# The last 64 rows of w_down as 128 half rows, in a one-token decoder block

## The chip, the core and the metric

The kernel runs on one core of a Trainium2 chip. A core has five instruction streams: TensorE (PE in the profile, with PEld for its weight loads), VectorE (DVE), ScalarE (ACT), GpSimd (POOL) and SyncE (SP), which here issues nearly all transfers. Sixteen DMA engines move the data between HBM and SBUF. The metric is the device time of one execution in microseconds, as the median of several runs. The kernel before took 206.41 us (three runs, 206.30 to 206.46).

## What is computed

One token (x, 640 values) goes through attention over a cache of 4096 positions in 32 heads, and then through a gated MLP with 1728 hidden columns:

```
h  = x + softmax(q k^T / sqrt(128)) v @ wo          q = layernorm(x) @ wq
g  = layernorm(h) @ w_gate                          w_gate, w_up: 640 x 1728
u  = layernorm(h) @ w_up
h2 = h + (gelu(g) * u) @ w_down                     w_down: 1728 x 640
```

All inputs are bfloat16. The caches are 64 of the 84 MB that are read; w_gate, w_up and w_down are 2.2 MB each.

## The kernel before

The kernel is written out by hand for the five engines. A small helper (class Sched) collects each engine's instructions in the order in which the code names them, with the semaphore waits of each; nothing is reordered after that. All large transfers stand in one queue, SP's, and are worked off in its order.

The first 170 us stream the caches. For eight groups of four heads, VectorE multiplies keys by the query (L296), TensorE folds the products (L305), VectorE reduces them (L312), ScalarE exponentiates (L344), and TensorE sums the values (L351). K and V have two buffers each; SP waits for a buffer to come free before it issues the next load (L222, L231).

The weights of the second half stand behind the caches in the same queue, into buffers that are free by then: wo in four pieces, w_gate and w_up in two each (L384), then w_down. 1728 hidden columns are 13 full slices of 128 and a remainder of 64 (FREM). L395 loads the remainder, 64 rows of w_down, on partitions 0 to 63 of slice 13 of wd_sb. L400 then loads the 13 full slices in four parts of 6, 4, 2 and 1 slices (WD_PARTS), each on 128 partitions; within a part of n slices, a partition holds n rows that follow each other in memory.

The MLP uses the hidden columns in the same layout. Function up (L444 to L457) multiplies five chunks of the 640 inputs by the 14 slices, 70 matmuls into one column of a PSUM tile for each slice, once for w_gate (pg) and once for w_up (pu). The remainder's matmuls have 64 columns of weights and fill rows 0 to 63 alone; the other rows of pg and pu are set to zero at the start (L192, L193). VectorE and ScalarE then form gelu(g) * u in hm, one column for each slice (L461 to L470).

The down projection (L472 to L480) takes 4 matmuls for each slice, one for each quarter of the 640 outputs, into four rows of pd (a PSUM tile that the profile calls pf). The remainder comes first, with 64 rows, then the 13 slices as their parts land. VectorE copies the result (L481), and SP stores it (L482).

TensorE runs its instructions in order, so a matmul that waits for a part of w_down holds up all behind it.

Of the kernel before, what the change touches and what calls it, by code (L numbers as in the profile page):

```python
# [5 lines left out]
FP32 = mybir.dt.float32  # L6
BF16 = mybir.dt.bfloat16
ALU = mybir.AluOpType
ACTF = mybir.ActivationFunctionType
AX = mybir.AxisListType  # L10

D = 640
# [3 lines left out]
DF = 1728  # L16
# [7 lines left out]
NG = H // HG  # L24
# [4 lines left out]
NFT = 13  # L29
NF = NFT + 1  # L30
WD_PARTS = (6, 4, 2, 1)
# [5 lines left out]
FREM = DF - NFT * 128  # L37
# [67 lines left out]
def bass_sequential_preLN__gqa_block_cached__glu_gated_geglu__decode_kernel(  # L105
# [12 lines left out]
    S = Sched(nc)  # L118

    def sb(name, shape, dt):  # L120
        return nc.alloc_sbuf_tensor(name, shape, dt)
# [7 lines left out]
    def over(name, base, shape):  # L129
        return nc.alloc_sbuf_tensor_at(name, shape, BF16, offset=nc.lookup_mloc(base).addr)  # L130
# [3 lines left out]
    wg_sb = over("wg_sb", kbuf[NG % 2], [128, NC_D, DF])  # L134
    wu_sb = over("wu_sb", kbuf[(NG + 1) % 2], [128, NC_D, DF])
    wd_sb = over("wd_sb", vbuf[NG % 2], [128, NF, D])
# [21 lines left out]
    hln = sb("hln", [128, NC_D], BF16)  # L158
# [6 lines left out]
    r_t = sb("r_t", [128, NF], FP32)  # L165
    gu = sb("gu", [128, NF], FP32)
    hm = sb("hm", [128, NF], BF16)
    o_sb = sb("o_sb", [128, D // 4], BF16)
    hx = sb("hx", [128, 32, NC_D], FP32)
    m32 = sb("m32", [128, 32], FP32)  # L170
# [3 lines left out]
    I32 = sb("I32", [128, 128], FP32)  # L174
# [8 lines left out]
    pz = nc.alloc_psum_tensor("pz", [128, 512], FP32)  # L183
    pg = nc.alloc_psum_tensor("pg", [128, 512], FP32)
    pu = nc.alloc_psum_tensor("pu", [128, 512], FP32)
# [3 lines left out]
    t_onebf = S.op("vector", lambda v: v.memset(ones_bf[:, :], 1.0))  # L189
    t_p4 = [S.op("vector", lambda v, i=i: v.memset(P4[i][:, :, :], 0.0)) for i in range(2)]  # L190
    t_rs = S.op("vector", lambda v: v.memset(RS[:, :], 0.0))
    t_pg = S.op("vector", lambda v: v.memset(pg[:, 0:NF], 0.0))  # L192
    t_pu = S.op("vector", lambda v: v.memset(pu[:, 0:NF], 0.0))  # L193
    t_i32 = S.op("gpsimd", lambda g: g.affine_select(
        I32[:, :], ones[:, :], pattern=[[1, 128]], compare_op=ALU.is_equal,
        fill=0.0, base=0, channel_multiplier=-1), [t_one])
# [3 lines left out]

    t_e4 = S.op("vector", lambda v: v.reduce_sum(
        e4[:, :], I32[:, :].rearrange("p (j i) -> p j i", j=4), axis=AX.X), [t_i32])
    t_m32 = S.op("vector", lambda v: v.reduce_sum(
        m32[:, :], I32[:, :].rearrange("p (j i) -> p i j", j=4), axis=AX.X))
    t_sel = None
# [13 lines left out]
    kfree, vfree = [None] * NG, [None] * NG  # L219
# [27 lines left out]
    def layernorm(src, t_src, o, dst, ps, beside=None):  # L247
        a = S.op("vector", lambda v: v.tensor_mul(sq[:, :], src[:, :], src[:, :]), [t_src])
        S.op("vector", lambda v: v.reduce_sum(st[:, o:o + 1], src[:, :], axis=AX.X))
        b = S.op("vector", lambda v: v.reduce_sum(st[:, o + 1:o + 2], sq[:, :], axis=AX.X), [a])  # L250
        c = S.op("tensor", lambda t: t.matmul(ps[:, 0:2], ones[:, :], st[:, o:o + 2],  # L251
                                              start=True, stop=True), [b, t_one])
        if beside is not None:
            beside()
        q = 6 * (o // 2)
        d = S.op("vector", lambda v: v.tensor_scalar(
            ln[:, q:q + 1], ps[:, 0:1], inv_d, 0.0, ALU.mult, ALU.add), [c])
        e = S.op("vector", lambda v: v.tensor_scalar(
            ln[:, q + 1:q + 2], ln[:, q:q + 1], ln[:, q:q + 1], -EPS, ALU.mult, ALU.add), [d])
        f = S.op("vector", lambda v: v.tensor_scalar(  # L260
            ln[:, q + 2:q + 3], ps[:, 1:2], inv_d, ln[:, q + 1:q + 2], ALU.mult, ALU.subtract), [e])
        k = S.op("scalar", lambda a: a.activation(ln[:, q + 3:q + 4], ln[:, q + 2:q + 3], ACTF.Ln), [f])  # L262
        m = S.op("scalar", lambda a: a.activation(
            ln[:, q + 4:q + 5], ln[:, q + 3:q + 4], ACTF.Exp, scale=-0.5), [k])
        return S.op("vector", lambda v: v.tensor_scalar(  # L265
            dst[0], dst[1], ln[:, q:q + 1], ln[:, q + 4:q + 5], ALU.subtract, ALU.mult), [m])
# [113 lines left out]
    def pieces(slot, dst, src, cuts, waits):  # L380
        toks = []
        for i in range(len(cuts) - 1):
            lo, hi = cuts[i], cuts[i + 1]
            tok = S.dma("sync", "%s%d" % (slot, i), lambda s, lo=lo, hi=hi: s.dma_start(  # L384
                dst[:, lo:hi, :], src[:, lo:hi, :]), waits)
            toks += [tok] * (hi - lo)
        return toks
# [3 lines left out]
    d_wg = pieces("wg", wg_sb, B_w_gate[:, :].rearrange("(p c) n -> p c n", c=NC_D),  # L391
                  [0, 3, 5], [kfree[NG - 2]])
    d_wu = pieces("wu", wu_sb, B_w_up[:, :].rearrange("(p c) n -> p c n", c=NC_D),
                  [0, 3, 5], [kfree[NG - 1]])
    d_wdr = S.dma("sync", "wdr", lambda s: s.dma_start(  # L395
        wd_sb[0:FREM, NFT, :], B_w_down[NFT * 128:DF, :]), [vfree[NG - 2]])
    d_wd = []
    for i, n in enumerate(WD_PARTS):
        s0 = len(d_wd)
# [10 lines left out]
    b = None  # L410
    for j in range(4):
        b = S.op("tensor", lambda t, j=j: t.matmul(
            pq[:, 0:32], sel[:, j, :], aH[:, 32 * j:32 * j + 32], start=(j == 0), stop=(j == 3)),
            [a, t_sel, t_qb[NG - 1]], token=(j == 3))
# [4 lines left out]
    for c in range(H):  # L419
        for cc in range(NC_D):  # L420
            last = c == H - 1 and cc == NC_D - 1
            b = S.op("tensor", lambda t, c=c, cc=cc, last=last: t.matmul(  # L422
                pp[:, cc:cc + 1], wo_sb[:, c, cc::NC_D], aP[:, c:c + 1],
                start=(c == 0 and cc == 0), stop=last, skip_group_check=True),
                [t_ap, d_wo[c]], token=last)
# [3 lines left out]
    pd = pf[1]  # L429
    NQ = D // 4  # L430
# [10 lines left out]
    t_hln = layernorm(h32, t_h, 2, (hln[:, :], h32[:, :]), pz, residual)  # L441


    def up(ps, w, d_w, t0):  # L444
        b = None
        for c in range(NC_D):
            for s in range(NF):
                first = c == 0 and s == 0
                last = c == NC_D - 1 and s == NF - 1
                rows, cols = FREM, slice(NFT * 128, DF)  # L450
                if s < NFT:
                    b0, n, k = WD_COLS[s]
                    rows, cols = 128, slice(b0 + k, b0 + 128 * n, n)
                b = S.op("tensor", lambda t, s=s, c=c, rows=rows, cols=cols, first=first, last=last: t.matmul(
                    ps[0:rows, s:s + 1], w[:, c, cols], hln[:, c:c + 1],
                    start=first, stop=last, skip_group_check=True), [t_hln, d_w[c], t0], token=last)
        return b  # L457

    t_g = up(pg, wg_sb, d_wg, t_pg)
    t_u = up(pu, wu_sb, d_wu, t_pu)  # L460
    a = S.op("vector", lambda v: v.tensor_copy(g_t[:, :], pg[:, 0:NF]), [t_g])  # L461
    a = S.op("vector", lambda v: v.tensor_mul(t1[:, :], g_t[:, :], g_t[:, :]), [a])
    a = S.op("vector", lambda v: v.tensor_mul(t2[:, :], t1[:, :], g_t[:, :]), [a])
    a = S.op("vector", lambda v: v.scalar_tensor_tensor(
        out=t3[:, :], in0=t2[:, :], scalar=GELU_C1, in1=g_t[:, :], op0=ALU.mult, op1=ALU.add), [a])
# [3 lines left out]
    a = S.op("vector", lambda v: v.tensor_mul(gu[:, :], g_t[:, :], r_t[:, :]), [a])  # L469
    t_hm = S.op("vector", lambda v: v.tensor_mul(hm[:, :], gu[:, :], pu[:, 0:NF]), [a, t_u])  # L470

    order = [NFT] + list(range(NFT))  # L472
    for i, s in enumerate(order):
        kk = FREM if s == NFT else 128
        for j in range(4):
            last = i == NF - 1
            b = S.op("tensor", lambda t, s=s, j=j, kk=kk, last=last: t.matmul(  # L477
                pd[32 * j:32 * j + 1, 0:NQ], hm[0:kk, s:s + 1], wd_sb[0:kk, s, j * NQ:(j + 1) * NQ],
                start=False, stop=last, skip_group_check=True),
                [t_hm, d_wd[s]], token=(last and j == 3))  # L480
    t_o = S.op("vector", lambda v: v.tensor_copy(o_sb[:, :], pd[:, 0:NQ]), [b])  # L481
    d_o = S.dma("sync", "out", lambda s: s.dma_start(  # L482
        out[0, 0, :].rearrange("(j i) -> j i", j=4), o_sb[0:128:32, :]), [t_o])
# [32 lines left out]
```

## Time and profile before

The profiled execution took 206.16 us, 0.25 us less than the median.

| | |
|---|---|
| median of the runs | 206.41 us |
| the profiled execution | 206.16 us |
| its span, first to last instruction | 204.9 us |
| busy: PE, DVE, ACT, POOL | 132.3, 103.4, 24.4, 2.2 us |
| bytes read from HBM | 84.23 MB, 411 GB/s over the span |
| L454 (up), 128 columns: weight load, matmul | 127 ns, 178 ns |
| L454 (up), 64 columns: weight load, matmul | 127 ns, 212 ns |
| L477 (down): weight load, matmul | 79 ns, 338 ns (medians) |
| L395 (remainder): issue, issue to landing | 0.62 us, 25.3 us |

Busy times of TensorE add up pipelined instructions, so its matmuls overlap. A row of a timeline gives the start, the duration, the engine, the line and the operation, and in brackets how long the engine sat idle before it and what ended that. The rows of DMA in slices are the share of time in which the core's 16 DMA engines were busy, and the GB/s that they moved.

### The profile page before, as it was taken

The numbers are of one execution on the slowest core, as the hardware profiler recorded it, in microseconds if no ns is written. First come the engines' busy times: TensorE is split into PE (matmuls) and PEld (weight loads), VectorE is DVE, ScalarE is ACT, GpSimd is POOL, SyncE is SP. The second block draws the span as 40 slices with busy tenths as digits, with TensorE's granted clock in tenths as the row PEclk, the third lists the DMA queues.
The fourth block names the chain that finished last, engine by engine and source line by source line (L and its number), as shares of the span: only waits on it lengthen the run. The fifth ranks groups of instructions, "written<-read, shape, count | busy, mean of one in ns | idle before, by whom it ended". The sixth has DMA issues, their size and how long they took to land.

```text
span 204.9 us, 3982 instructions
## 1 busy us (share of the span) xinstructions
PE 132.3 (65%) x1847; PEld 77.5 (38%) x1847; DVE 103.4 (50%) x118; ACT 24.4 (12%) x86; POOL 2.2 (1%) x11
## 2 busy tenths in 40 slices
PE   0003057656897668785968478858776958676884
PEld 0002012222562363254326223713272228676672
DVE  2003088699579537935772777187627950101120
ACT  2001000040230040022005000500040004000000
POOL 3000000000000000000000000000000000000000
PEclk9999999999979955995799579757975797555555
DMA  7999999999999999999999999999999999999991
GB/s 256 432 432 409 416 486 422 416 416 457 448 413 416 429 453 429 416 419 440 435 435 422 413 441 448 419 419 429 441 448 419 400 413 431 429 402 421 405 358 62
DMA packets 4712, 84.48 MB, mean 412 GB/s; under 512 B 664, under 2 KB 856, under 8 KB 1880
## 3 DMA queue, kind: packets, MB, share of 16 engines
q1 hardware_dynamic: 4552, 84.23, 96.8%
q8 instruction: 14, 0.23, 0.5%
q10 hardware_dynamic: 144, 0.00, 0.0%
q14 instruction: 2, 0.02, 0.0%
HBM read 84.23 MB, written 0.00 MB: 411 GB/s over the span
## 4 chain that ended last, share of the span: by engine, by line
DMA 61%; DVE 20%; PE 13%; SPq 4%; issue 1%
DMA kbuf<-in_A_k_cache_dram 50%; DVE prod L296 16%; DMA wd_sb<-in_B_w_down_dram 10%; PE pf L305 10%; SPq L400 4%; DVE sc L312 4%; PE po L351 2%; PE pm L331 0%; PE pf L477 0%; DVE mx L329 0%; PE pz L370 0%; PE pm L337 0%; SPq L212 0%; DVE mrow L334 0%; DVE o_sb L481 0%
## 5 line engine op out<-in xcount | busy, mean ns | idle before, releaser
L305 PE MATMUL pf<-prod,Ibf 128*128 128x512 bf16 x256 | 73.9, 447 | 36.8 <-DVE prod L296 36.7
L296 DVE TENSOR_TENSOR prod<-kbuf,qb 128x4096 bf16<-128x4096 bf16 x32 | 72.4, 2282 | 27.5 <-DMA kbuf<-in_A_k_cache_dram 26.9
L305 PEld LDWEIGHTS pf<-prod,Ibf 128*128 128x128 bf16 x256 | 26.5, 111 | 81.1 <-DVE prod L296 45.9
L312 DVE TENSOR_REDUCE sc<-pf 128x32 f32<-128x512 f32 x32 | 21.9, 686 | 21.6 <-PE pf L305 21.6
L351 PE MATMUL po<-P,vbuf 128*128 128x4 bf16 x1024 | 27.9, 165 | 1.6 <-issue 1.6
L351 PEld LDWEIGHTS po<-P,vbuf 128*128 128x128 bf16 x1024 | 27.4, 100 | 1.8 <-issue 1.7
L344 ACT ACTIVATE P<-sc,nb 32x128 bf16<-32x128 f32 x32 | 18.6, 580 | 0.9
L285 ACT CAST qb<-pq 128x128 bf16<-128x128 f32 x8 | 2.1, 265 | 103.4 <-PE pq L281 103.4
L251 PE MATMUL pz<-st,ones 128*128 128x2 f32 x4 | 1.2, 364 | 17.5 <-DVE st L250 17.5
L422 PE MATMUL pf<-aP,wo_sb 128*128 128x1 bf16 x160 | 7.0, 179 | 2.3 <-issue 1.8
L344 ACT ACTIVATION_READ_ACCUMULATOR P<-sc,nb 32x1 f32 x32 | 8.1, 253 | 0.0
L422 PEld LDWEIGHTS pf<-aP,wo_sb 128*128 128x128 bf16 x160 | 6.7, 131 | 2.6 <-issue 2.0
L251 PEld LDWEIGHTS pz<-st,ones 128*128 128x128 f32 x4 | 1.0, 313 | 17.6 <-DVE st L250 17.6
L268 DVE CAST x<-x_sb 128x5 f32<-128x5 bf16 x1 | 0.2, 171 | 13.9 <-DMA x_sb<-in_A_x_dram 13.9
L281 PE MATMUL pq<-wq_sb,xb 128*32 128x128 bf16 x160 | 5.7, 232 | 1.7 <-DVE xb L265 1.7
L331 PE MATMUL pm<-I,mx 128*1 128x128 f32 x16 | 3.0, 271 | 4.6 <-DVE mx L329 4.6
L281 PEld LDWEIGHTS pq<-wq_sb,xb 128*32 128x32 bf16 x160 | 4.2, 100 | 4.8 <-issue 3.0
L337 PE MATMUL pm<-mrow,ones 1*128 1x4 f32 x16 | 3.0, 258 | 3.0 <-DVE mrow L334 3.0
L426 DVE TENSOR_TENSOR h<-x,pf 128x5 f32<-128x5 f32 x1 | 0.2, 161 | 9.1 <-PE pf L422 9.1
L262 ACT ACTIVATE ln<-ln 128x1 f32<-128x1 f32 x2 | 0.4, 202 | 35.0 <-DVE ln L260 35.0
L340 ACT ACTIVATE nb<-pm 128x4 f32<-128x4 f32 x8 | 1.4, 173 | 26.5 <-PE pm L337 26.5
L337 PEld LDWEIGHTS pm<-mrow,ones 1*128 1x128 f32 x16 | 2.3, 182 | 5.3 <-DVE mrow L334 5.3
(59 smaller groups left out, 38.2 us busy)
## 6 DMA issues: line engine op xcount, KB each, us to landing
kbuf<-in_A_k_cache_dram SPq DMA_DIRECT2D x8, 4096.0 KB, 27.1
vbuf<-in_A_v_cache_dram SPq DMA_DIRECT2D x7, 4096.0 KB, 29.3
wq_sb<-in_A_wq_dram SPq DMA_DIRECT2D x1, 5120.0 KB, 15.2
wo_sb<-in_A_wo_dram SPq DMA_DIRECT2D x2, 1920.0 KB, 26.6
vbuf<-in_A_v_cache_dram SPq DMA_DIRECT2D x1, 2048.0 KB, 16.0
vbuf<-in_A_v_cache_dram SPq DMA_DIRECT2D x1, 1536.0 KB, 19.3
wg_sb<-in_B_w_gate_dram SPq DMA_DIRECT2D x1, 1296.0 KB, 32.5
wu_sb<-in_B_w_up_dram SPq DMA_DIRECT2D x1, 1296.0 KB, 30.1
```

The costliest lines, as they stand in the source:

```text
L251: c = S.op("tensor", lambda t: t.matmul(ps[:, 0:2], ones[:, :], st[:, o:o + 2], start=True, stop=True), [b, t_one])
L281: tok = S.op("tensor", lambda t, hh=hh, c=c, n0=n0: t.matmul(pq[hh * PPH:(hh + 1) * PPH, 0:DH], xb[:, c, :], wq_sb[:, c, n0:n0 + DH], star ...
L285: t_qb[g] = S.op("scalar", lambda a: a.copy(qb[:, g, :], pq[:, 0:DH]), [tok])
L296: return S.op("vector", lambda v: v.tensor_tensor(out=prod[n % NPR][:, :, :], in0=kbuf[g % 2][:, s * RP:(s + 1) * RP, :], in1=qb[:, g, :]. ...
L305: fold_done[n] = S.op("tensor", lambda t, j=j: t.matmul(pf[n % 2][:, :], Ibf[:, :], prod[n % NPR][:, :, j * W:(j + 1) * W], start=(j == 0) ...
L312: red_done[n] = S.op("vector", lambda v: v.reduce_sum(sc[g % 2][:, s * RP:(s + 1) * RP], pf[n % 2][:, :].rearrange("p (r w) -> p r w", r=R ...
L331: b = S.op("tensor", lambda t: t.matmul(pm[0:1, 0:128], mx[:, g:g + 1], I32[:, :], start=True, stop=True), [a, t_i32, t_exp[g - 1] if g el ...
L337: d = S.op("tensor", lambda t: t.matmul(pm[:, 256:256 + HG], ones[0:1, :], mrow[0:1, g * HG:(g + 1) * HG], start=True, stop=True), [c])
L344: t_exp[g] = S.op("scalar", lambda a, lo=lo, hi=hi, h=h, hh=hh: a.activation(P4[g % 2][lo:hi, :, hh], sc[g % 2][lo:hi, :], ACTF.Exp, bias= ...
L351: t_pv[g] = S.op("tensor", lambda t, r=r: t.matmul(po[:, g * HG:(g + 1) * HG], vbuf[g % 2][:, r, :], P4[g % 2][:, r, :], start=(r == 0), s ...
L400: tok = S.dma("sync", "wd%d" % i, lambda s, s0=s0, n=n: s.dma_start(wd_sb[:, s0:s0 + n, :], B_w_down[128 * s0:128 * (s0 + n), :].rearrange ...
L422: b = S.op("tensor", lambda t, c=c, cc=cc, last=last: t.matmul(pp[:, cc:cc + 1], wo_sb[:, c, cc::NC_D], aP[:, c:c + 1], start=(c == 0 and ...
```

## The change

The remainder of w_down is loaded as 128 half rows of 320 values: row r's first half lies on partition 2r, its second half on partition 2r+1. So that the hidden columns can meet it there, the remainder's slice in up is now 128 columns wide: it takes the last 128 columns of w_gate and w_up, of which the first 64 belong to slices that are there already. All rows of pg and pu are now written, and the memsets at the start go.

Of the last column of hm, rows 64 to 127 hold the remainder's 64 values. A new matmul with a 0/1 matrix (twice) puts each of them on two neighbouring partitions, in a column of pz. A multiply on VectorE with a parity mask (hpar) makes two columns of it, hr: one with zeros on odd partitions, one with zeros on even ones. The first goes with the two quarters of the output that the first half rows hold, the second with the other two. The four matmuls of the remainder now come after the first part's 24, not ahead of them.

```diff
--- before.py
+++ after.py
@@ -165,6 +165,9 @@
     r_t = sb("r_t", [128, NF], FP32)
     gu = sb("gu", [128, NF], FP32)
     hm = sb("hm", [128, NF], BF16)
+    hr = sb("hr", [128, 2], BF16)
+    hpar = sb("hpar", [128, 2], FP32)
+    twice = sb("twice", [128, FREM, 2], BF16)
     o_sb = sb("o_sb", [128, D // 4], BF16)
     hx = sb("hx", [128, 32, NC_D], FP32)
     m32 = sb("m32", [128, 32], FP32)
@@ -189,8 +192,6 @@
     t_onebf = S.op("vector", lambda v: v.memset(ones_bf[:, :], 1.0))
     t_p4 = [S.op("vector", lambda v, i=i: v.memset(P4[i][:, :, :], 0.0)) for i in range(2)]
     t_rs = S.op("vector", lambda v: v.memset(RS[:, :], 0.0))
-    t_pg = S.op("vector", lambda v: v.memset(pg[:, 0:NF], 0.0))
-    t_pu = S.op("vector", lambda v: v.memset(pu[:, 0:NF], 0.0))
     t_i32 = S.op("gpsimd", lambda g: g.affine_select(
         I32[:, :], ones[:, :], pattern=[[1, 128]], compare_op=ALU.is_equal,
         fill=0.0, base=0, channel_multiplier=-1), [t_one])
@@ -200,6 +201,10 @@
 
     t_e4 = S.op("vector", lambda v: v.reduce_sum(
         e4[:, :], I32[:, :].rearrange("p (j i) -> p j i", j=4), axis=AX.X), [t_i32])
+    S.op("vector", lambda v: v.reduce_sum(
+        hpar[:, :], I32[:, :].rearrange("p (r h) -> p h r", h=2), axis=AX.X))
+    t_tw = S.op("vector", lambda v: v.tensor_copy(
+        twice[:, :, :], I32[:, 128 - FREM:128].unsqueeze(2).to_broadcast([128, FREM, 2])))
     t_m32 = S.op("vector", lambda v: v.reduce_sum(
         m32[:, :], I32[:, :].rearrange("p (j i) -> p i j", j=4), axis=AX.X))
     t_sel = None
@@ -393,7 +398,7 @@
     d_wu = pieces("wu", wu_sb, B_w_up[:, :].rearrange("(p c) n -> p c n", c=NC_D),
                   [0, 3, 5], [kfree[NG - 1]])
     d_wdr = S.dma("sync", "wdr", lambda s: s.dma_start(
-        wd_sb[0:FREM, NFT, :], B_w_down[NFT * 128:DF, :]), [vfree[NG - 2]])
+        wd_sb[:, NFT, 0:D // 2], B_w_down[NFT * 128:DF, :].rearrange("r (h n) -> (r h) n", h=2)), [vfree[NG - 2]])
     d_wd = []
     for i, n in enumerate(WD_PARTS):
         s0 = len(d_wd)
@@ -441,23 +446,23 @@
     t_hln = layernorm(h32, t_h, 2, (hln[:, :], h32[:, :]), pz, residual)
 
 
-    def up(ps, w, d_w, t0):
+    def up(ps, w, d_w):
         b = None
         for c in range(NC_D):
             for s in range(NF):
                 first = c == 0 and s == 0
                 last = c == NC_D - 1 and s == NF - 1
-                rows, cols = FREM, slice(NFT * 128, DF)
+                part = w[:, c, DF - 128:DF]
                 if s < NFT:
                     b0, n, k = WD_COLS[s]
-                    rows, cols = 128, slice(b0 + k, b0 + 128 * n, n)
-                b = S.op("tensor", lambda t, s=s, c=c, rows=rows, cols=cols, first=first, last=last: t.matmul(
-                    ps[0:rows, s:s + 1], w[:, c, cols], hln[:, c:c + 1],
-                    start=first, stop=last, skip_group_check=True), [t_hln, d_w[c], t0], token=last)
+                    part = w[:, c, b0 + k:b0 + 128 * n:n]
+                b = S.op("tensor", lambda t, s=s, c=c, part=part, first=first, last=last: t.matmul(
+                    ps[:, s:s + 1], part, hln[:, c:c + 1],
+                    start=first, stop=last, skip_group_check=True), [t_hln, d_w[c]], token=last)
         return b
 
-    t_g = up(pg, wg_sb, d_wg, t_pg)
-    t_u = up(pu, wu_sb, d_wu, t_pu)
+    t_g = up(pg, wg_sb, d_wg)
+    t_u = up(pu, wu_sb, d_wu)
     a = S.op("vector", lambda v: v.tensor_copy(g_t[:, :], pg[:, 0:NF]), [t_g])
     a = S.op("vector", lambda v: v.tensor_mul(t1[:, :], g_t[:, :], g_t[:, :]), [a])
     a = S.op("vector", lambda v: v.tensor_mul(t2[:, :], t1[:, :], g_t[:, :]), [a])
@@ -469,15 +474,24 @@
     a = S.op("vector", lambda v: v.tensor_mul(gu[:, :], g_t[:, :], r_t[:, :]), [a])
     t_hm = S.op("vector", lambda v: v.tensor_mul(hm[:, :], gu[:, :], pu[:, 0:NF]), [a, t_u])
 
-    order = [NFT] + list(range(NFT))
+    b = S.op("tensor", lambda t: t.matmul(
+        pz[:, 32:33], twice[:, :, :], hm[:, NFT:NF], start=True, stop=True), [t_hm, t_tw])
+    t_hr = S.op("vector", lambda v: v.tensor_tensor(
+        out=hr[:, :], in0=hpar[:, :], in1=pz[:, 32:33].to_broadcast([128, 2]), op=ALU.mult), [b])
+
+    def down(s, j):
+        if s == NFT:
+            return hr[:, j // 2:j // 2 + 1], wd_sb[:, NFT, j % 2 * NQ:(j % 2 + 1) * NQ]
+        return hm[:, s:s + 1], wd_sb[:, s, j * NQ:(j + 1) * NQ]
+
+    order = list(range(WD_PARTS[0])) + [NFT] + list(range(WD_PARTS[0], NFT))
     for i, s in enumerate(order):
-        kk = FREM if s == NFT else 128
         for j in range(4):
             last = i == NF - 1
-            b = S.op("tensor", lambda t, s=s, j=j, kk=kk, last=last: t.matmul(
-                pd[32 * j:32 * j + 1, 0:NQ], hm[0:kk, s:s + 1], wd_sb[0:kk, s, j * NQ:(j + 1) * NQ],
+            b = S.op("tensor", lambda t, s=s, j=j, last=last: t.matmul(
+                pd[32 * j:32 * j + 1, 0:NQ], *down(s, j),
                 start=False, stop=last, skip_group_check=True),
-                [t_hm, d_wd[s]], token=(last and j == 3))
+                [t_hr if s == NFT else t_hm, d_wd[s]], token=(last and j == 3))
     t_o = S.op("vector", lambda v: v.tensor_copy(o_sb[:, :], pd[:, 0:NQ]), [b])
     d_o = S.dma("sync", "out", lambda s: s.dma_start(
         out[0, 0, :].rearrange("(j i) -> j i", j=4), o_sb[0:128:32, :]), [t_o])

```

twice and hpar are built from the identity matrix at the start. The order of the transfers in SP's queue, the number of bytes and the other parts of w_down stay as they were.

## The prediction

> **What bounds the kernel now.** I read the page's slices first, then the chain of waits, then the last microseconds as a timeline, and last the DMA rate in stretches.
>
> ```profile
> span 204.9 us, 3982 instructions
> ...
> DMA  7999999999999999999999999999999999999991
> ...
> q1 hardware_dynamic: 4552, 84.23, 96.8%
> q8 instruction: 14, 0.23, 0.5%
> ```
>
> The DMA row is full from the second slice to the next to last: 84 MB go in without a pause, and engines' work counts only where no transfer covers it. The end of the chain of waits says which transfer the end hangs on:
>
> ```profile
> 180.74 21.34 DMA wd_sb<-in_B_w_down_dram
> 202.12 0.73 PE pf L477 x12
> 202.87 0.32 DVE o_sb L481
> ```
>
> The last parts of w_down are on their way for 21 us, then 12 matmuls, a copy and the store end the kernel. The timeline of the tail shows how far each engine is from that path:
>
> ```profile
> 198.80 0.17 DVE L470 TENSOR_TENSOR hm<-gu,pu 128x14 bf16<-128x14 f32 x1 [2.05 <-PE pu L454]
> 199.02 0.09 PEld L477 LDWEIGHTS pf<-wd_sb,hm 64*1 64x1 bf16 x4 [0.42 <-DVE hm L470]
> 199.03 0.30 PE L477 MATMUL pf<-wd_sb,hm 64*1 64x160 bf16 x4 [0.33 <-DVE hm L470]
> 199.78 0.63 PEld L477 LDWEIGHTS pf<-wd_sb,hm 128*1 128x1 bf16 x24 [0.67 <-DMA wd_sb<-in_B_w_down_dram]
> ...
> 201.31 0.36 PEld L477 LDWEIGHTS pf<-wd_sb,hm 128*1 128x1 bf16 x16 [0.90 <-DMA wd_sb<-in_B_w_down_dram]
> ...
> 202.12 0.10 PEld L477 LDWEIGHTS pf<-wd_sb,hm 128*1 128x1 bf16 x8 [0.45 <-DMA wd_sb<-in_B_w_down_dram]
> 202.52 0.09 PEld L477 LDWEIGHTS pf<-wd_sb,hm 128*1 128x1 bf16 x4 [0.30 <-DMA wd_sb<-in_B_w_down_dram]
> ```
>
> Each of the four parts of w_down (6, 4, 2 and 1 slices) lets TensorE wait: 0.67, 0.90, 0.45 and 0.30 us. So the end moves only if the last part lands at another time. When it lands is a matter of the rate, in stretches:
>
> ```profile
> core 0: us, PE busy (x) PEld busy (x) DVE busy (x) ACT busy (x) POOL busy (x), PEclk, DMA share, GB/s
> 185.00:193.50 8.50, 6.05 (x114) 5.18 (x113) 1.40 (x8) 0.41 (x2) 0.47 (x1) 0.50 1.01 418
> 193.50:195.50 2.00, 2.00 (x43) 1.93 (x42) 0.42 (x3) 0.00 (x0) 0.00 (x0) 0.50 1.04 359
> 195.50:196.50 1.00, 1.00 (x21) 0.96 (x19) 0.65 (x4) 0.22 (x1) 0.00 (x0) 0.50 0.96 391
> 196.50:197.50 1.00, 0.99 (x21) 0.89 (x21) 0.22 (x2) 0.00 (x0) 0.00 (x0) 0.50 0.98 330
> ...
> 198.00:198.50 0.50, 0.50 (x14) 0.48 (x14) 0.00 (x0) 0.00 (x0) 0.00 (x0) 0.50 1.09 435
> ```
>
> The DMA engines are busy all through (0.96 to 1.04), but from 193.5 to 195.5 and again from 196.5 to 197.5 they move 359 and 330 GB/s instead of 418. The trace's records of single packets say the same: for 40 us before, a packet takes its size's usual time within 2%, save where an instruction fetch shares its engine; in these two stretches every packet on every engine takes 1.1 to 1.5 times that. Both stretches follow the transfer that the change remakes, the 64 rows of L395: its 64 packets of 1280 B start from 192.9 to 195.0 on eleven engines and from 196.2 to 196.7 on the other five, each time some 0.5 us before the dip. The last part of w_down has packets of 1280 B too, on 128 partitions (198.3 us on): there the rate is 435 and the packets take their usual 55 ns. So size is not the cause; what sets this transfer apart is that it writes 64 partitions.
>
> **The change part by part.**
> *The transfer of the last rows.* Same 80 KB at the same place in the queue, as 128 packets of 640 B over all partitions. What the dips cost now: (418-359)x2 + (418-391)x1 + (418-330)x1 = 233 KB not moved, or 0.56 us at 418 GB/s. From the packet records, the six engines that end last lost 0.48 to 0.58 us of packet time in the dips; I take 0.50, since those set the end. If the dips go, the last landing moves from 202.47 to about 201.97. If the partitions are not their cause, the gain is 0.
> Against it stands the smaller packet. Packets of 320, 1280 and 2560 B take 18, 55 and 102 ns in the records, those of one engine following at 3 ns less; 640 B interpolates to 30. Each engine then spends 8x27 = 216 ns instead of 4x52 = 208: +0.01 us. The bounds are 8x18 = 144 (a 320 B packet's price, -0.06) and 8x52 = 416 (a 1280 B packet's, +0.21). I take +0.02, since both neighbours lie on one line.
>
> [...]
> [...]
>
> *The queue.* On SP nothing is passed or reordered; the one instruction has twice the packets. SP's issues of L400 already stretch to 5.69 us behind a full queue, so the four behind it may be issued later: four more packets per engine are at most half of an eight-packet part, and the parts ahead of it land 2 to 5 us apart, so up to 2.5 us. The last is issued at 182.6 and lands 19.9 us later; this is hidden by the queue's depth, at zero, and would cost only beyond that.
> *The up projections.* Ten of 140 matmuls have 128 columns instead of 64. By form the two weight loads take 127 ns each, the matmuls 178 and 212 (the narrow ones longer): between -10x0.034 and +0.05 us, taken as 0, as TensorE is done at 198.7 and waits for the first part until 199.78. With the gain that part lands near 199.25, and the path below still comes first.
> *The new matmul and multiply.* After hm (198.97) TensorE duplicates the last column into pz: one weight load and matmul, by L454's rows about 0.25 us, where the four narrow matmuls stood (0.30). It ends by 199.3; behind it on PE stand the 24 of the first part, delayed by at most 0.05 us. VectorE's product of two columns from pz costs 0.16 to 0.22 us (L256 and L260, which read pz), so hr is there by 199.6. Nothing else stands behind it on DVE until L481. The four matmuls that need it now come after the 24, which take 0.97 us and end near 200.3: 0.7 us of slack. They then run 0.30 us to 200.6, before the second part's landing at about 200.8. If this cover of 0.2 us were gone, the 16 behind them would start late, with 0.8 us to the third part's landing to make it up.
> *Start.* Two memsets of 0.07 us go; a reduction (0.27 to 0.37, as L201 and L203) and a copy of 128x128 (0.17 to 0.44, as L188 and L265) come. DVE idles 13.91 us until x lands at 16.2: zero.
>
> *Sum.* -0.50 + 0.02 = -0.48 us. The profiled execution took 206.16 (span 204.9, 1.26 around it): 205.68. The median of the three runs is 0.25 higher, so 206.41 - 0.48 = 205.93. The bounds: -0.56 - 0.06 = -0.62 and, with nothing gained and the dear packet, +0.21.
>
> **The rivals.**
> *The dips stay* (the source side or the start of w_down's stream makes them). For it: the engines read the same 5 KB pieces from the same places, and the packets of the first part of w_down start only 0.2 us after those of the rows. Against it: engines stay on that first part from 195.5 to 196.5 at 391, and the next dip awaits the five late engines' packets of the remainder. Time 206.41 + 0.02 = 206.43.
> *They go only in part*, say to the 0.19 us that 80 KB take at 418 GB/s: one such transfer's own time. Time 206.24. Against it: all engines slow, for over 2 us in all.
> *Half rows are dear and the dips stay:* 640 B at the 1280 B price, 206.62.
> *Slower: an instruction fetch on a late engine.* Queue 8's 14 fetches of 16 KB each hold one DMA engine 1.0 to 1.1 us (packet records). The one at 199.06 falls on an engine that would have ended 1.1 us before the last. The change puts two instructions into TensorE's stream just there; if the fetch falls on one of the five last engines instead, the last landing is 1.1 us later: -0.48 + 1.09 = +0.6, 207.0. It decides as soon as the engine that is hit has less than 0.6 us (1.09 - 0.48) of lead. Against it: the stream up to that point has the same instructions, so the same engine should be next.
>
> **How the numbers follow.** A measurement tells 0.2% (0.41 us) from no change. Dips gone: 0.66, own range 205.65 to 206.1, of it 0.50 beyond 0.41 us and 0.16 short of it. In part: 0.11. Stay: 0.14. Dear half rows: 0.04. Fetch: 0.05. Faster is 0.50, same 0.16 + 0.11 + 0.14 + 0.04 = 0.45, slower 0.05. The range runs from 205.65 to 206.5: it takes in the dips that stay (206.43) and leaves out the last two cases and the far tails.
>
> **What would show it.** Right: from 193.5 to 197.5 the rate stays near 418; the last weight load of the down projection starts near 202.0 instead of 202.52, its four waits remain, and the four matmuls of the half rows start without one for DVE. Wrong: 330 to 360 GB/s in the same stretches (partitions aren't the cause); a wait for hr in TensorE's row; or a late landing with an undisturbed rate (a fetch on a late engine). The prediction is most at risk where the gain is real but 0.3 us, just short of what can be told.

## The result

The changed kernel takes 205.77 us (median of nine runs, 205.55 to 206.00), the kernel before 206.28 in runs beside it. The ratio is 0.9974 with a 95% interval of 0.9964 to 0.9984: 0.54 us faster, between 0.33 and 0.74. The forecast was 205.93, 0.48 us faster.

First the DMA rate of the changed kernel, in the stretches in which the kernel before had its two dips. The last column is GB/s.

```profile
core 0: us, PE busy (x) PEld busy (x) DVE busy (x) ACT busy (x) POOL busy (x), PEclk, DMA share, GB/s
185.00:193.50 8.50, 6.08 (x131) 5.29 (x130) 1.40 (x8) 0.41 (x2) 0.47 (x1) 0.50 1.02 422
193.50:195.50 2.00, 1.30 (x35) 1.22 (x34) 1.15 (x7) 0.22 (x1) 0.00 (x0) 0.50 0.99 410
195.50:196.50 1.00, 0.78 (x23) 0.70 (x21) 0.14 (x1) 0.00 (x0) 0.00 (x0) 0.50 1.07 437
196.50:197.50 1.00, 0.84 (x21) 0.85 (x22) 0.00 (x0) 0.00 (x0) 0.00 (x0) 0.50 0.99 412
```

The dips are gone: 410, 437 and 412 GB/s where 359, 391 and 330 stood. Reckoned as in the prediction, (422-410)x2 + (422-437)x1 + (422-412)x1 = 19 KB or 0.05 us are left of the 0.56.

Then the tail of the changed kernel as a timeline:

```profile
197.96 0.17 DVE L475 TENSOR_TENSOR hm<-gu,pu 128x14 bf16<-128x14 f32 x1 [2.33 <-PE pu L459]
198.19 0.10 PEld L477 LDWEIGHTS pz<-hm,twice 128*128 128x128 bf16 x1 [0.41 <-DVE hm L475]
198.41 0.16 DVE L479 TENSOR_TENSOR hr<-hpar,pz 128x2 bf16<-128x2 f32 x1 [0.28 <-PE pz L477]
199.20 0.63 PEld L491 LDWEIGHTS pf<-wd_sb,hm 128*1 128x1 bf16 x24 [0.91 <-DMA wd_sb<-in_B_w_down_dram]
199.82 0.14 PEld L491 LDWEIGHTS pf<-wd_sb,hr 128*1 128x1 bf16 x4
...
200.74 0.36 PEld L491 LDWEIGHTS pf<-wd_sb,hm 128*1 128x1 bf16 x16 [0.78 <-DMA wd_sb<-in_B_w_down_dram]
...
201.56 0.10 PEld L491 LDWEIGHTS pf<-wd_sb,hm 128*1 128x1 bf16 x8 [0.46 <-DMA wd_sb<-in_B_w_down_dram]
201.94 0.09 PEld L491 LDWEIGHTS pf<-wd_sb,hm 128*1 128x1 bf16 x4 [0.28 <-DMA wd_sb<-in_B_w_down_dram]
```

The four waits for parts of w_down remain (0.91, 0.78, 0.46 and 0.28 us). The last weights are loaded from 201.94 instead of 202.52, and all behind them has moved along. The new steps lie where they were expected to: hr is there at 198.57, and the matmuls that need it start at 199.82 without a wait. The whole span is 0.6 us shorter (204.3). Not all of that is the dips: hln already began 0.16 us sooner here, 190.75 against 190.91, before the remainder's first packet, and the profiled execution, at 205.56 us, is near the lowest of the nine.

### The profile page after: what moved, and what is told of

Read it like the earlier page. It is cut to its first block, busy times and chain, and to the rows that moved or that the text cites. A ratio compares the mean times of both kernels' runs of the same rounds, so it can differ in the third digit from the quotient of the medians.

```text
span 204.3 us, 3985 instructions
## 1 busy us (share of the span) xinstructions
PE 130.1 (64%) x1848; PEld 76.0 (37%) x1848; DVE 103.8 (51%) x119; ACT 24.4 (12%) x86; POOL 2.2 (1%) x11
## 4 chain that ended last, share of the span: by engine, by line
DMA 61%; DVE 21%; PE 13%; SPq 4%; issue 1%
DMA kbuf<-in_A_k_cache_dram 50%; DVE prod L301 16%; PE pf L310 10%; DMA wd_sb<-in_B_w_down_dram 10%; SPq L405 4%; DVE sc L317 4%; PE po L356 2%; PE pm L336 0%; PE pf L491 0%; DVE mx L334 0%; PE pz L375 0%; SPq L217 0%; PE pm L342 0%; DVE o_sb L495 0%; DVE mrow L339 0%
```

## Experiments

Three things could have made the dips: the partitions that the 64 rows go to; the place that they are read from, or the beginning of w_down's stream; and the number of packets, four on an engine instead of eight. In the change itself these go together. So the first four kernels are a control and three that differ from it in one operand of one DMA.

**Control, and the same rows on other partitions.** The control leaves out the remainder's matmuls:

```diff
-    order = [NFT] + list(range(NFT))
+    S.wait("tensor", d_wdr)
+    order = list(range(NFT))
...
-            last = i == NF - 1
+            last = i == NFT - 1
```

> The kernel before with the remainder's four down matmuls left out (the output lacks the last 64 hidden columns); the 64 rows are still loaded on partitions 0 to 63, and TensorE waits for them. It is the control of the three that follow. Both theories: as the kernel before, within 0.1 us (206.2 to 206.4), since those four matmuls (0.30 us) stood in a wait for the first part; the rate between 193.5 and 197.5 us falls to 330 to 360 GB/s as before.

It measured 206.31 us, ratio 1.0002 (0.9993 to 1.0011), with 369 and 330 GB/s in the two stretches:

```profile
193.50:195.50 2.00, 1.30 (x27) 1.17 (x25) 0.70 (x4) 0.07 (x1) 0.00 (x0) 0.50 1.03 369
196.50:197.50 1.00, 0.99 (x20) 0.86 (x17) 0.00 (x0) 0.00 (x0) 0.00 (x0) 0.50 1.01 330
```

The next three differ from it in one line each:

```diff
-        wd_sb[0:FREM, NFT, :], B_w_down[NFT * 128:DF, :]), [vfree[NG - 2]])
+        wd_sb[32:32 + FREM, NFT, :], B_w_down[NFT * 128:DF, :]), [vfree[NG - 2]])
```

> As the control, with the same 64 packets of 1280 B from the same source put on partitions 32 to 95. Theory of the partitions (0 to 63 alone are a bad target, 32 to 95 reach both halves): the dips go, as in the changed kernel, 0.50 us less than the control, about 205.8. Theory of the source (the 5 KB pieces that are read, or the start of w_down's stream): nothing changes, 206.3, with the dips. Theory of the count (four packets for an engine in place of eight): nothing changes either.

205.74 us, ratio 0.9971 (0.9959 to 0.9982): the whole gain of the change, without any of its other parts.

```diff
-        wd_sb[0:FREM, NFT, :], B_w_down[NFT * 128:DF, :]), [vfree[NG - 2]])
+        wd_sb[FREM:128, NFT, :], B_w_down[NFT * 128:DF, :]), [vfree[NG - 2]])
```

> As the control, on partitions 64 to 127. Theory of the partitions: this is the other half, as lopsided as the first; the dips stay, 206.3, 360 and 330 GB/s. If only partitions 0 to 63 are special, the dips go: 205.8. Theories of the source and of the count: 206.3.

206.35 us, ratio 1.0005 (0.9996 to 1.0014): no gain.

```diff
-        wd_sb[0:FREM, NFT, :], B_w_down[NFT * 128:DF, :]), [vfree[NG - 2]])
+        wd_sb[0:128:2, NFT, :], B_w_down[NFT * 128:DF, :]), [vfree[NG - 2]])
```

> [...] If what counts is that the rows are spread over all partitions, the dips go: 205.8. [...] Source and count: 206.3.

205.74 us, ratio 0.9971 (0.9960 to 0.9982): the whole gain again.

The rates of the two stretches go with the times. On partitions 32 to 95:

```profile
185.00:193.50 8.50, 6.73 (x131) 5.84 (x129) 1.40 (x8) 0.41 (x2) 0.47 (x1) 0.50 1.01 420
193.50:195.50 2.00, 1.62 (x31) 1.48 (x29) 0.70 (x4) 0.21 (x1) 0.00 (x0) 0.50 1.01 421
196.50:197.50 1.00, 1.00 (x25) 0.97 (x23) 0.00 (x0) 0.00 (x0) 0.00 (x0) 0.50 1.03 426
```

On partitions 64 to 127:

```profile
185.00:193.50 8.50, 6.28 (x120) 5.41 (x119) 1.40 (x8) 0.41 (x2) 0.47 (x1) 0.50 1.02 419
193.50:195.50 2.00, 1.44 (x31) 1.31 (x29) 0.70 (x4) 0.01 (x1) 0.00 (x0) 0.50 1.02 353
196.50:197.50 1.00, 1.00 (x21) 0.93 (x18) 0.00 (x0) 0.00 (x0) 0.00 (x0) 0.50 0.98 320
```

On the even partitions:

```profile
193.50:195.50 2.00, 1.90 (x41) 1.76 (x39) 0.57 (x4) 0.00 (x0) 0.00 (x0) 0.50 1.02 427
196.50:197.50 1.00, 1.00 (x25) 0.97 (x24) 0.06 (x1) 0.00 (x0) 0.00 (x0) 0.50 1.03 426
```

Source, size and number of packets are the same in all four. With the rows on one half of the partitions, the lower or the upper, the rate in these two stretches falls to 320 to 370 GB/s; with rows in both halves it stays above 420. The packet records agree: in these stretches 121 of 183 packets of the control took over 1.1 times what is usual for their size outside of them, and 128 of 176 with the rows on partitions 64 to 127, but none of 218 on 32 to 95 and none of 225 on the even ones. That settles it for the partitions and against the other two. It is not the number of partitions that counts, 64 in all four, but that they lie in both halves. Why the halves count, the four runs do not show.

**The wide projections alone.** This kernel has the change's new up and the later place of the remainder's matmuls, but loads whole rows on partitions 64 to 127, where the last 64 rows of hm's last column stand anyway:

```diff
-        wd_sb[:, NFT, 0:D // 2], B_w_down[NFT * 128:DF, :].rearrange("r (h n) -> (r h) n", h=2)), [vfree[NG - 2]])
+        wd_sb[FREM:128, NFT, :], B_w_down[NFT * 128:DF, :]), [vfree[NG - 2]])
...
-            return hr[:, j // 2:j // 2 + 1], wd_sb[:, NFT, j % 2 * NQ:(j % 2 + 1) * NQ]
+            return hm[FREM:128, s:s + 1], wd_sb[FREM:128, s, j * NQ:(j + 1) * NQ]
```

(against the changed kernel; twice, hpar, hr and the matmul into pz are gone too)

> One part of the change alone: the last slice of w_gate and w_up 128 columns wide, the remainder's matmuls after the first part, but the 64 rows loaded whole, on partitions 64 to 127, so that hm needs no duplication. All the work is done. If the gain comes from the partitions of the transfer alone: no gain, 206.35, with dips to about 355 and 320 GB/s, while up is done about 0.9 us sooner per projection (2.8 us in place of 3.7, as in the changed kernel). If the quicker up or the later place of the remainder's matmuls had a share in the gain: below 206.2.

206.36 us, ratio 0.9999 (0.9991 to 1.0008): no gain. Its timeline:

```profile
190.84 2.74 PE L452 MATMUL pg<-hln,wg_sb 128*128 128x1 bf16 x70 [0.91 <-DVE hln L263]
...
194.95 1.71 PE L452 MATMUL pu<-hln,wu_sb 128*128 128x1 bf16 x42 [1.37 <-DMA wu_sb<-in_B_w_up_dram]
...
197.33 1.19 PE L452 MATMUL pu<-hln,wu_sb 128*128 128x1 bf16 x28 [0.67 <-DMA wu_sb<-in_B_w_up_dram]
```

In the kernel before, the same two projections ran without a wait between them:

```profile
191.26 3.71 PE L454 MATMUL pg<-hln,wg_sb 128*128 128x1 bf16 x70 [0.91 <-DVE hln L265]
194.91 3.79 PE L454 MATMUL pu<-hln,wu_sb 128*128 128x1 bf16 x70
```

The 70 matmuls of w_gate take 2.74 us instead of 3.71. What TensorE saves it then waits for w_up, 1.37 and 0.67 us. So this part of the change is worth nothing by itself. By the code the half rows did not call for it either: with the narrow slice the remainder's values stand in rows 0 to 63 of hm's last column, and a 0/1 matrix that picks these rows would do. No run tries that.

**Twice the transfer.** The rows are loaded a second time, to a slot that nothing reads, on the lower half and then on partitions 32 to 95 (the remainder's matmuls are left out in both):

```diff
+    d_wdr2 = S.dma("sync", "wdr2", lambda s: s.dma_start(
+        wd_sb[0:FREM, NF, :], B_w_down[NFT * 128:DF, :]), [vfree[NG - 2]])
```

> The control (remainder's matmuls left out) with the 64 rows loaded twice, to two slots, both on partitions 0 to 63: 80 KB more, 0.19 us at 418 GB/s. If each such transfer costs its dip: 206.3 + 0.19 + 0.50 to 0.65 = 207.0 to 207.15. If the dips come with the first of them alone (a beginning, not a load): 206.5.

207.51 us, ratio 1.0051 (1.0037 to 1.0065): more than either theory allowed.

> The same, both on partitions 32 to 95: only the bytes are more, so 205.75 + 0.19 = 205.95 on every theory that is left, with no dips; 206.3 or more if two such transfers disturb each other.

205.94 us, ratio 0.9983 (0.9974 to 0.9991): 0.20 us over the single load there, about what 80 KB take at 418 GB/s (0.19 us). So one load on the lower half costs 206.31 - 205.74 = 0.57 us more than the same load on both halves, and two cost 207.51 - 205.94 = 1.57 us more. By the medians that is more than twice 0.57. Four of the five runs of the kernel with two lower loads say so too; the fifth, at 207.00, would give 1.06. The rates of the two kernels, the lower half first:

```profile
193.50:195.50 2.00, 1.97 (x40) 1.81 (x39) 0.09 (x1) 0.00 (x0) 0.00 (x0) 0.50 1.04 289
195.50:196.50 1.00, 1.00 (x23) 0.97 (x24) 0.62 (x5) 0.21 (x1) 0.00 (x0) 0.50 0.90 278
197.50:198.50 1.00, 0.50 (x10) 0.41 (x10) 0.00 (x0) 0.00 (x0) 0.00 (x0) 0.50 0.96 210
```

```profile
193.50:195.50 2.00, 2.00 (x42) 1.93 (x41) 0.36 (x3) 0.00 (x0) 0.00 (x0) 0.50 1.03 426
195.50:196.50 1.00, 1.00 (x22) 0.94 (x20) 0.65 (x4) 0.21 (x1) 0.00 (x0) 0.50 0.98 402
197.50:198.50 1.00, 1.00 (x24) 0.96 (x23) 0.00 (x0) 0.00 (x0) 0.00 (x0) 0.50 0.99 397
```

**Narrower targets, and less at a time.** The rows on 16 partitions, four on each (one packet of 5 KB for each engine):

```diff
-        wd_sb[0:FREM, NFT, :], B_w_down[NFT * 128:DF, :]), [vfree[NG - 2]])
+        wd_sb[0:16, NFT:NFT + 4, :], B_w_down[NFT * 128:DF, :].rearrange("(p i) n -> p i n", i=4)), [vfree[NG - 2]])
```

> The control with the 64 rows on partitions 0 to 15, four on each. [...] If the loss is a fixed one of a transfer that isn't spread over all partitions: 206.3.

206.31 us, ratio 0.9998 (0.9990 to 1.0007): no dearer than 64 partitions. A loss that grows as the target gets narrower did not show. The shape of the loss is another, though: 371 GB/s in the first stretch and 284 in the second, where the control has 369 and 330.

> The 64 rows loaded twice to partitions 0 to 15 (remainder's matmuls left out). One load there lost no more than one to 0 to 63 (206.31 in both), two loads to 0 to 63 lost 1.2 us more than one. If what is lost is set by the bytes of one transfer and not by how narrow the target is: as the two loads to 0 to 63, 207.5. If a backlog at the target counts, which is deeper at the narrower one: over 208.

207.48 us, ratio 1.0058 (1.0046 to 1.0071): as much as two loads on 64 partitions, 207.51. Four times narrower cost nothing more at either size. The packets are four times larger here, 5 KB instead of 1280 B, so the two were not varied apart.

The rows as two loads of 32, one for each half:

```diff
-        wd_sb[0:FREM, NFT, :], B_w_down[NFT * 128:DF, :]), [vfree[NG - 2]])
+        wd_sb[0:32, NFT, :], B_w_down[NFT * 128:NFT * 128 + 32, :]), [vfree[NG - 2]])
+    d_wdr2 = S.dma("sync", "wdr2", lambda s: s.dma_start(
+        wd_sb[64:96, NFT, :], B_w_down[NFT * 128 + 32:DF, :]), [vfree[NG - 2]])
```

> The control with the 64 rows as two loads of 32, the first to partitions 0 to 31, the second to 64 to 95: every half is lopsided, the whole is not. If what counts is the balance within one transfer: dips in both, together about as before, 206.3. If 40 KB at a time are few enough to be taken up without a jam, or if the engines' loads mix: less than that, down to 205.75.

206.19 us, ratio 0.9992 (0.9983 to 1.0001), with 379, 417 and 362 GB/s in the three stretches. The dips are shallower, but most of the loss is there, 0.45 us over the load on 32 to 95: two lopsided loads behind each other do not make a balanced one.

## Why the prediction was right

- *The dips are the cost, and the 64 partitions make them.* Right in that the target makes them, and now shown rather than inferred: moving the same 64 packets to both halves brings the whole gain (205.74), moving them to the other half none (206.35). But it is not that the transfer writes 64 partitions, which the prediction named as what sets it apart: 32 to 95 are 64 too. Nor was every packet in the two stretches slowed: 121 of 177 took over 1.1 times their usual time, 35 at most 1.05 times. Nor did all packets of the 40 us before keep to 2% of their usual time: 103 of the 1426 over 4 B that start from 152.0 to 192.5 us are further than that from the median of their size, 40 of them over 5% above it.
- *Their size.* 0.50 us was taken, with 0.48 to 0.58 from the packet records and 0.56 from the rates. The partitions alone measure 0.57 (control less partitions 32 to 95), the change 0.54. This size was read off the trace before, not worked out from a cause. The packet records show where it lies: the remainder's own 64 packets took 55 to 74 ns, together 0.13 us over the usual 55, while the 7680 B packets of w_down's first part beside them took 358 ns (median in the two stretches) instead of 291. In the changed kernel that median is 291. So in these records the loss falls almost wholly on what runs beside the lopsided transfer. The rivals "the dips stay" and "in part" fall with this.
- *The price of half rows.* Interpolated 30 ns a packet; the records of the changed kernel have 32, for every one of the 128, first and second halves of a row alike. The whole change is at 205.77, whole rows on partitions 32 to 95 at 205.74, so the half rows and the two new instructions cost no more than what the runs can tell.
- *SP's queue.* Hidden, as said: the part behind the half rows now takes 4.28 us to issue (2.01 before), yet all four take 10.25 us together (10.26 before), and the last part still lands 19.5 us after its issue (19.9 before). At that issue 1173 packets over 4 B were still to end, 1101 before the change.
- *Duplication and product.* Hidden, as said: 0.16 us for the product, no wait for hr, 1.25 us between the two.
- *The up projections.* The one term that was mis-sized. Their ten wider matmuls were put between -0.34 and +0.05 us together. In fact the 64-column ones had held up the stream: the 70 matmuls of w_gate take 2.76 us instead of 3.71, those of w_up 2.92 instead of 3.79. In the records a 64-column matmul starts 95 ns after the one ahead of it, and the one behind it 142 to 147 ns later; for the wide one in its place both are 26 to 28 ns. The by-form rows from which the bound was made show durations of single pipelined instructions, not what one costs the stream. It had no effect on the forecast, since TensorE then waits longer for w_up and w_down; the kernel with that part alone is at 206.36.
- *An instruction fetch on a late engine.* Did not happen: the last weight load moved by 0.58 us along with the dips.

How the loss grows stays open. Twice the bytes lost 2.8 times as much by the medians, a target four times narrower the same, two half-sized loads most of it. The packets' time over the usual from 193 to 199 us, as a mean of the 16 engines, goes the same way in the one traced execution of each: 0.56 us in the control, 1.63 and 1.60 with two loads (0 to 63, 0 to 15), 0.39 with the two half-sized ones, and 0.03 or less wherever each load reaches both halves. Why two loads lose more than twice one is not shown by any of these runs.

## What to carry to other kernels

Read a DMA-bound kernel's rate in stretches of a microsecond or two, next to what is issued there: here engines with a busy share of 0.98 moved 330 GB/s where 418 had been usual, a loss that the busy share does not show. A transfer in such a stream that filled only the lower or upper 64 partitions slowed the transfers beside it, here by 0.57 us for 80 KB; 64 rows were free of that when they reached both halves, on partitions 32 to 95 or on every other one. Those two runs leave out the remainder's matmuls, so no run here shows a whole kernel with that simpler layout. Where the matmul needs its operand in another place, the compute for it can hide behind the stream (here 0.19 us on TensorE and 0.16 us on VectorE, done 1.25 us before it was needed), and it is the layout of the operand, not the count of its bytes, that one should be ready to change.

## What was not expected

- A matmul with 64 columns of weights among those with 128 cost the stream some 0.19 us more than a wide one: (3.71 - 2.76) / 5 for each of the five in a projection, though its own weight load was listed at 127 ns like all others.
- Loads on 16 partitions, in packets of 5 KB, were no dearer than on 64 in packets of 1280 B (206.31 and 206.31 once, 207.48 and 207.51 twice).
